# A cosine attention and feed-forward kernel: the first batch's row sums in 32-column tiles, and a new written order for the first three batches

## Chip, cores and metric

The kernel runs on one core of one Trainium2 chip. The time is device microseconds of that core, and a kernel's time is the median of its runs. Of its engines, TensorE (PE; PEld is its weight loads) does the matmuls, VectorE (DVE), ScalarE (ACT) and GpSimd (POOL) the element-wise work, and DMA queues, issued from SyncE (SP), GpSimd and ScalarE, move data between DRAM and the on-chip memories SBUF and PSUM (the matmuls' accumulators).

## What is computed

Attention over normalised queries and keys, then a feed-forward layer with an exact gelu. There are 8 batches, 12 heads, 448 rows and a head width of 64; the 3584 output rows have 768 features and the hidden layer has 2048.

```python
q_n = q / (np.linalg.norm(q, axis=-1, keepdims=True) + 1e-06)
k_n = k / (np.linalg.norm(k, axis=-1, keepdims=True) + 1e-06)
scores = np.matmul(q_n, k_n.transpose(0, 1, 3, 2)) / tau        # tau = 0.1
attn = np.exp(scores - np.max(scores, axis=-1, keepdims=True))
attn = attn / (np.sum(attn, axis=-1, keepdims=True) + 1e-09)
x = np.matmul(attn, v)                                          # 8, 12, 448, 64
x = x.transpose(0, 2, 1, 3).reshape(3584, 768)
h = x @ w_in                                                    # 768 x 2048
g = 0.5 * h * (1.0 + erf(h / sqrt(2)))
out = g @ w_out                                                 # 2048 x 768
```

## The kernel before

**Tiling.** Heads are taken four at a time: a group g is 4 heads of one batch, so a batch has three groups and the kernel 24 (batch 0 is groups 0 to 2, batch 1 groups 3 to 5, batch 2 groups 6 to 8). A group's 448 rows are cut into C = 7 chunks of 64. Two heads lie on the two halves of the 128 partitions; s counts the two pairs of heads of a group. The preparation of q and k goes by units: group 0 is two units (one pair each, tiles of 128x448), every later group one (128x896), so unit u is group u - 1 from u = 2 on.

**A unit's preparation.** `load_qk` (line 127) brings q and k of a group with DMAs on SP (one of group 0's goes on ScalarE's queue) into one of four buffers of the tag `qk`. `square` (line 166) squares q or k on the engine that its call names (AC ScalarE, DV VectorE, GP GpSimd), `reduce` (line 177) sums the squares on VectorE, `logs` and `roots` (lines 187, 192) take the square root on ScalarE as Exp of half of Ln, for one unit or for two at once (the list `groups`, line 118), `inverses` (line 197) adds the small constant and inverts on VectorE, and `scale` (line 211) multiplies q or k by the inverse norm and rounds to bf16 (`qkb`), again on the engine named. A buffer `qk` is free for a later load when both its scalings are done. `transposes` (line 225) turns `qkb` into `qkT`: on TensorE with a copy by VectorE (`copies`) for the first units, as a transposing DMA on SP for the later ones.

**A group's attention.** `scores` (line 247) is 4 matmuls for each chunk into a pair of PSUM banks, `exps` (line 261) one exponential on ScalarE for such a pair, 128x896. `sums` (line 316) lets TensorE sum the exponentials over the keys with a matrix of ones, `turned`, `inverted` and `spread` (lines 352, 357, 373) turn these sums, invert them and spread them over the partitions on VectorE. `values` (line 335) is exponentials times v on TensorE, and `normalise` (line 378) writes x, the product with the inverse sums, as input of the first layer. Of some groups (`folded` on GpSimd, `gather` on VectorE) the sums are taken by adding the exponentials' chunks instead.

The row sums have two forms. For batch 0 a matmul gives 64 columns of output, which hold the sums of a pair of heads twice over:

```python
nc.tensor.matmul(bank_t[g, "sm"][64 * s:64 * (s + 1), :S],
                 lhsT=ones2.rearrange("p a h r -> p (a h r)"), rhs=pt_t[g, s, c],
                 start=(c == 0), stop=(c == C - 1), tile_position=(0, 64 * s))
```

For the others it gives 32, so that four such tiles, two for each pair, lie side by side in TensorE's array. Each of a pair's two tiles then holds a part of the chunks, and chunk 2 is split by columns; `inverted` adds the parts with four small reduces and one more before the reciprocal.

**The feed-forward layer.** For each batch and each of 16 blocks m of the hidden layer, `mm(b, m, k0, k1)` (line 517) multiplies x by w_in over 6 steps k (products `hp`), and `gelu` (line 520) writes g on ScalarE. `run(n)` (line 503) emits the next n steps of the second layer: an output piece is 128 rows by 384 columns, 16 steps of 4 matmuls each, and then a reduce on VectorE and, every second piece, a store on SP. Batch 0 has six such pieces, batch 1 eight; they stand in the list `todo_t`, filled by `more(b)` from `output_pieces(b)` (line 1373). The weights come through GpSimd's DMA queue: `load_wi` (line 462) in four calls of two DMAs (k 0 and 1; k 2 and 3; k 4 and 5 in two halves), `load_wo` (line 471) in four quarters, and v with `load_v` (line 142).

**The order.** The kernel is recorded with a manual schedule: each engine and each queue executes its instructions in the order in which the Python text issues them. `opening()` (line 538) is a list of some 690 calls, one step each, that fixes this for batches 0, 1 and 2 up to batch 2's attention and the scores of groups 9 and 10. `spin` (line 486) is filler matmuls on TensorE, `table` (line 500) loads ScalarE's function table (one for exponentials and logarithms, one for gelu), `banks`, `bank` and `bank_o` choose PSUM banks. After it `first(2)` and, for b from 3 to 7, `attention(b, ...)` and `first(b)` are loops.

## Time and profile before

| | us |
|---|---|
| runs | 393.38, 390.82, 391.53 |
| their median | 391.53 |
| span of the profiled execution | 390.6 |

The profiled execution is near the fastest of the runs. The granted TensorE clock is full speed throughout. The page's cut of the span into 40 equal slices of 9.8 us shows, in tenths, how busy each engine was in each.

```profile
PE   7899999999999999999999999999999999999996
DVE  4878439876778896879696896889685993670032
ACT  5895789857999958996678767997577646504300
POOL 4796950557998399969594794969595770910000
DMA  8999999926899691889067490876045600130033
```

TensorE is below nine tenths only in the first two slices and the last; the DMA engines are full in the first eight. The page's list of the costliest groups tells what fills the engines; its columns are the line, the engine, the operation, output and input, shapes and count, then the busy time and the mean of one in ns, then the idle time before and what ended it.

```profile
L427 PE MATMUL op<-wo,g 64*64 64x384 bf16 x3456 | 167.1, 323 | 0.2 <-issue 0.2
L267 ACT ACTIVATE pt<-st 128x896 bf16<-128x896 f32 x168 | 147.2, 918 | 19.6 <-PE st L257 17.5
L493 PE MATMUL hp<-x,wi 128*128 128x448 bf16 x768 | 147.0, 353 | 0.0
L219 POOL TENSOR_TENSOR qkb<-qk,rn 128x896 bf16<-128x896 f32 (+1 forms) x49 | 80.4, 1662 | 46.0 <-DVE rn L203 37.9
L175 POOL TENSOR_TENSOR sq<-qk 128x896 f32<-128x896 f32 x16 | 26.6, 1685 | 23.8 <-DMA qk<-in_q_dram 13.3
L173 ACT ACTIVATE sq<-qk 128x896 f32<-128x896 f32 (+1 forms) x33 | 28.8, 901 | 4.4 <-DMA qk<-in_q_dram 3.2
```

### The profile page before, as it was taken

What the parts mean: (1) busy time and instruction counts of PE and PEld (TensorE: products, weight loads), DVE (VectorE), ACT (ScalarE), POOL (GpSimd) and SP (SyncE); (2) the same over time, 40 slices, a digit from 0 to 9 for tenths busy, and PEclk for the clock granted to TensorE, in tenths of its full rate; (3) what the DMA queues carried; (4) which work ended last, traced back from release to release, by engine and by line L of the source; (5) the groups of instructions that cost most, each with busy time, mean ns of one, the idle gap of its engine ahead of it and who ended that gap; (6) DMA issues with size and microseconds to landing.
All of it is one profiled execution on the core that took longest, in us unless ns stands there. A gap on an engine that the chain in (4) does not pass through costs nothing.

```text
span 390.6 us, 13166 instructions
## 1 busy us (share of the span) xinstructions
PE 382.6 (98%) x5820; PEld 236.6 (61%) x5820; DVE 273.0 (70%) x509; ACT 269.9 (69%) x391; POOL 248.7 (64%) x161
## 2 busy tenths in 40 slices
PE   7899999999999999999999999999999999999996
PEld 3444568555777656865567556775567555655674
DVE  4878439876778896879696896889685993670032
ACT  5895789857999958996678767997577646504300
POOL 4796950557998399969594794969595770910000
PEclk9999999999999999999999999999999999999999
DMA  8999999926899691889067490876045600130033
GB/s 265 264 262 229 176 191 329 254 56 157 179 203 299 112 217 69 185 158 275 5 172 130 120 243 2 185 131 118 3 91 81 154 9 2 44 82 2 7 79 83
DMA packets 64473, 54.85 MB, mean 140 GB/s; under 512 B 38688, under 2 KB 60320, under 8 KB 64416
## 3 DMA queue, kind: packets, MB, share of 16 engines
q1 hardware_dynamic: 54464, 41.79, 42.0%
q0 software_dynamic: 9568, 11.80, 18.5%
q8 instruction: 45, 0.74, 0.8%
q10 hardware_dynamic: 384, 0.43, 0.4%
q14 instruction: 12, 0.10, 0.1%
HBM read 45.61 MB, written 11.01 MB: 145 GB/s over the span
## 4 chain that ended last, share of the span: by engine, by line
PE 95%; DMA 2%; SPq 1%; ACT 1%; issue 0%; DVE 0%; ACTq 0%
PE hp L493 37%; PE op L427 36%; PE st L257 9%; PE o L346 8%; DMA qk<-in_k_dram 2%; PE op L451 1%; PE sm L323 1%; PE sm L332 1%; PE tp L236 1%; SPq L134 1%; ACT sq L173 0%; ACT pt L267 0%; PE spin L489 0%; DVE last L454 0%; ACT root L195 0%
## 5 line engine op out<-in xcount | busy, mean ns | idle before, releaser
L427 PE MATMUL op<-wo,g 64*64 64x384 bf16 x3456 | 167.1, 323 | 0.2 <-issue 0.2
L267 ACT ACTIVATE pt<-st 128x896 bf16<-128x896 f32 x168 | 147.2, 918 | 19.6 <-PE st L257 17.5
L493 PE MATMUL hp<-x,wi 128*128 128x448 bf16 x768 | 147.0, 353 | 0.0
L427 PEld LDWEIGHTS <-g 64*64 64x64 bf16 x3456 | 106.2, 107 | 40.9 <-issue 4.2
L493 PEld LDWEIGHTS <-wi 128*128 128x128 bf16 x768 | 74.3, 98 | 71.6 <-issue 3.2
L219 POOL TENSOR_TENSOR qkb<-qk,rn 128x896 bf16<-128x896 f32 (+1 forms) x49 | 80.4, 1662 | 46.0 <-DVE rn L203 37.9
L278 POOL TENSOR_TENSOR acc<-acc,pt 128x896 f32<-128x896 f32 x55 | 103.8, 1888 | 4.3
L436 DVE TENSOR_REDUCE ot<-op 128x384 f32<-128x768 f32 x50 | 47.3, 946 | 54.7 <-PE op L427 47.5
L1357 ACT ACTIVATE g<-hp 128x448 bf16<-128x448 f32 x96 | 46.2, 547 | 55.1 <-PE hp L493 55.1
L257 PE MATMUL st<-qkT 64*64 64x448 bf16 x672 | 62.8, 352 | 0.5 <-ACT pt L267 0.5
L183 DVE TENSOR_REDUCE nq<-sq 128x14 f32<-128x896 f32 (+1 forms) x50 | 50.4, 1036 | 13.6 <-ACT sq L173 7.1
L380 DVE TENSOR_TENSOR x<-o,rs 128x448 bf16<-128x448 f32 x48 | 27.6, 611 | 22.9 <-PE o L346 21.9
L175 POOL TENSOR_TENSOR sq<-qk 128x896 f32<-128x896 f32 x16 | 26.6, 1685 | 23.8 <-DMA qk<-in_q_dram 13.3
L346 PE MATMUL o<-pt,v 64*64 64x448 bf16 x672 | 39.5, 349 | 0.0
L290 DVE TENSOR_TENSOR acc<-acc,pt 128x896 f32<-128x896 f32 x30 | 33.0, 1099 | 1.0
L173 ACT ACTIVATE sq<-qk 128x896 f32<-128x896 f32 (+1 forms) x33 | 28.8, 901 | 4.4 <-DMA qk<-in_q_dram 3.2
L257 PEld LDWEIGHTS <-qkT 64*64 64x64 bf16 x672 | 23.1, 106 | 11.7 <-issue 3.7
L375 DVE STREAM_TRANSPOSE rs<-rc 128x448 f32<-128x448 f32 x48 | 28.1, 621 | 0.4
L278 POOL TENSOR_TENSOR acc<-pt 128x896 f32<-128x896 bf16 x11 | 20.7, 1878 | 10.9 <-ACT pt L267 10.9
L346 PEld LDWEIGHTS <-v 64*64 64x64 bf16 x672 | 21.1, 107 | 9.2 <-issue 0.2
L522 ACT ACTIVATE g<-hp 128x448 bf16<-128x448 f32 x32 | 15.4, 547 | 12.8 <-PE hp L493 12.7
L295 DVE TRANSPOSE_TENSOR_REDUCE sa<-acc 128x28 f32<-128x896 f32 x17 | 18.8, 1104 | 0.2
(54 smaller groups left out, 176.0 us busy)
## 6 DMA issues: line engine op xcount, KB each, us to landing
qk<-in_q_dram SPq DMA_DIRECT2D x23, 448.0 KB, 4.9
qk<-in_k_dram SPq DMA_DIRECT2D x23, 448.0 KB, 5.8
out_dram<-ot SPq DMA_DIRECT2D x48, 192.0 KB, 4.0
v<-in_v_dram POOLq DMA_DIRECT2D x6, 672.0 KB, 7.2
wo<-in_moe_w_out_dram POOLq DMA_DIRECT2D x4, 768.0 KB, 10.6
...
out_dram<-ot SPq DMA_DIRECT2D x12, 96.0 KB, 2.1
wi<-in_moe_w_in_dram POOLq DMA_DIRECT2D x4, 256.0 KB, 14.1
```

What stands on the lines that cost most here:

```text
L173: eng.activation(sq, t, AF.Square)
L183: nc.vector.tensor_reduce(nq_t[n][:, j, i], sq_t[g, i][:, s0:s1], mybir.AxisListType.X, ALU.add)
L219: eng.tensor_tensor(qkb[:, i, :, s0:s1].rearrange("p c s d -> p s c d"), t[:, i, s0:s1], rn[:, i].to_broadcast([128, s1 - s0, C, D]), ALU. ...
L257: nc.tensor.matmul(st[cols, n, :S], lhsT=qkT[rows, 1, c, cols], rhs=qkT[rows, 0, :, cols], start=True, stop=True, tile_position=(64 * s, 6 ...
L267: nc.scalar.activation(pt, st[:, :, :S], AF.Exp, scale=inv_tau)
L278: nc.gpsimd.tensor_tensor(acc_t[g], all_t[g][:, 0] if c == 1 else acc_t[g], all_t[g][:, c], ALU.add)
L290: nc.vector.tensor_tensor(acc_t[g], acc_t[g], all_t[g][:, c], ALU.add)
L346: nc.tensor.matmul(bank_t[g, h][cols, :S], lhsT=v_t[g][rows, s, c, :], rhs=pt_t[g, s, c][rows], start=(c == 0), stop=(c == C - 1), tile_po ...
L427: nc.tensor.matmul(ps[cols, r, :NH], lhsT=g_t[sb][rows, kf, t * 128 + 64 * c:t * 128 + 64 * (c + 1)], rhs=wo[rows, kf, ni * NH:(ni + 1) * NH],
L436: nc.vector.tensor_reduce(part, ps[:, :, :NH].rearrange("p r d -> p d r"), mybir.AxisListType.X, ALU.add)
L493: nc.tensor.matmul(t, lhsT=wi[:, kd, m * 128:(m + 1) * 128], rhs=x_t[b][:, kd, :], start=(kd == 0), stop=(kd == KD - 1))
L1357: nc.scalar.activation(g_t[sb][:, m, hf * S:(hf + 1) * S], hps.pop(m), AF.Gelu)
```

## The change

**Row sums.** The matrix `ones2` and the 64-column form go; batch 0's groups use the 32-column form and its longer `inverted`: 48 matmuls of 128x32 in place of 42 of 128x64, and for each of three groups five small reduces more on VectorE.

```diff
-                if g < NQ:
-                    nc.tensor.matmul(bank_t[g, "sm"][64 * s:64 * (s + 1), :S],
-                                     lhsT=ones2.rearrange("p a h r -> p (a h r)"), rhs=pt_t[g, s, c],
-                                     start=(c == 0), stop=(c == C - 1), tile_position=(0, 64 * s))
-                    continue
...
-        if g < NQ:
-            su = tr[:, :, :, 0]
-        else:
...
+        for j in range(4):
+            o = j ^ 1
+            nc.vector.tensor_reduce(tr[32 * j:32 * (j + 1), :, :, 1], tr[32 * o:32 * (o + 1), :, :, 0:1],
+                                    mybir.AxisListType.X, ALU.add)
+        su = rcp.tile([128, 2, NB], F32, tag="su", name=f"su{g}")
+        nc.vector.tensor_reduce(su, tr[:, :, :, 0:2], mybir.AxisListType.X, ALU.add)
```

**Two output pieces in turn.** Batch 0's first two pieces take 12 steps each, then their last four each, so that the last quarter of w_out is read from the 25th step on, not from the 13th.

```diff
+        pieces = [second_pieces(sb, t, ni) for t, ni in todo if t not in tail]
+        if b == 0:
+            n = KF * 3 // 4
+            one, two = pieces[:2]
+            pieces[:2] = [one[:n] + two[:n] + one[n:] + two[n:]]
+        fill = [f for p in pieces for f in p]
```

**Norms, buffers, a gather.** Units 5 and 6 (groups 4 and 5), whose logs, roots and inverses were taken together, get them one at a time. `gate(4)` gives group 4 the second of the four `qk` buffers, ahead of group 1's load, with a memset of two elements on GpSimd; group 3's load then takes the buffer that group 0 had, and group 5's the one that group 1 had. In `gather`, which batch 1's first group alone uses, each call names the engine of its chunk; chunk 2 is GpSimd's now, the others stay VectorE's.

```diff
+    groups[NQ + 2] = [NQ + 2]
+    NR = len(groups)
+    groups.append([NQ + 3])
...
+    def gate(g):
+        qk_t[g] = qkp.tile([128, 2, 2, C, D], F32, tag="qk", name=f"qk{g}")
+        nc.gpsimd.memset(qk_t[g][:, :, 0, 0, 0:1], 0.0)
...
-    def gather(g, c):
+    def gather(g, parts):
+        (eng, c), = parts
         if c == 1:
-            acc_t[g] = accp.tile([128, 2, S], F32, tag="acc", name=f"acc{g}")
-        nc.vector.tensor_tensor(acc_t[g], all_t[g][:, 0] if c == 1 else acc_t[g], all_t[g][:, c], ALU.add)
+            pool, tag, name = (sqp, "sq", f"sq{g}_2") if g == NQ + 1 else (accp, "acc", f"acc{g}")
+            acc_t[g] = pool.tile([128, 2, S], F32, tag=tag, name=name)
+        eng.tensor_tensor(acc_t[g], all_t[g][:, 0] if c == 1 else acc_t[g], all_t[g][:, c], ALU.add)
```

**The list `opening()`.** All of its calls stand in a new order, some 830 of them now, since most `run` calls are of one step. Squares and scalings have other engines: ScalarE has 31 squares (33 before), GpSimd 14 (16) and VectorE 5 (1); GpSimd has 41 scalings (49) and VectorE 9 (1). The first lines show the kind.

```diff
     def opening():
         load_qk(0)
-        table(EXP_SET)
+        banks(0, 6, 1)
+        square(0, ((DV, K),))
         square(0, ((AC, Q),))
...
```

What that makes of an engine is read from its own row of instructions. In the rows below a name's first number is the group (of squares `sq` the group and then 0 for q, 1 for k; of `lq`, `nq`, `se`, `rn` the unit or pair of units whose norms it holds; of `pt` and `st` the group of an exponential or score); a last number after an underscore is the buffer's.

ScalarE before, from its fourth square on:

```order
L173 ACTIVATE sq0_1_174<-qk0_133 128x448
L173 ACTIVATE sq1_0_194<-qk1_139 128x896
L190 ACTIVATE lq1_199<-nq1_184,tiny_121 128x14
L195 ACTIVATE root2_1_126<-lq1_199 128x14
L173 ACTIVATE sq1_1_217<-qk1_139 128x896
L173 ACTIVATE sq2_0_233<-qk2_142 128x896
L173 ACTIVATE sq2_1_238<-qk2_142 128x896
L190 ACTIVATE lq2_271<-nq2_201,tiny_121 128x28
L195 ACTIVATE root2_0_125<-lq2_271 128x28
L267 ACTIVATE pt0_281<-st0_0_255 128x2x448
L267 ACTIVATE pt0_281<-st0_2_273 128x2x448
```

ScalarE in the change, from its first square on:

```order
L177 ACT_TABLE_LOAD
L177 ACTIVATE sq0_0_139<-qk0_131 128x448
L496 ACT_TABLE_LOAD
L194 ACTIVATE lq0_166<-nq0_141,tiny_117 128x14
L199 ACTIVATE root2_0_121<-lq0_166 128x14
L177 ACTIVATE sq0_1_137<-qk0_131 128x448
L194 ACTIVATE lq1_200<-nq1_168,tiny_117 128x14
L199 ACTIVATE root2_1_122<-lq1_200 128x14
L177 ACTIVATE sq1_0_222<-qk1_146 128x896
L177 ACTIVATE sq1_1_257<-qk1_146 128x896
L177 ACTIVATE sq2_0_260<-qk2_150 128x896
L271 ACTIVATE pt0_262<-st0_0_235 128x2x448
```

Group 2's second square (`sq2_1`), its logs and roots, which stood ahead of the first exponential, are gone from there; two squares of group 0, one of them now VectorE's and one GpSimd's, too; the first exponential follows group 2's first square directly.

GpSimd before, from its first load of v:

```order
L155 DMA v0_180<-in_v_dram 128x2x448
L467 DMA wi_131<-in_moe_w_in_dram 64x2x2048 x2
L219 TENSOR_TENSOR qkb0_197<-qk0_133,rn0_192 128x7x64 x2
L219 TENSOR_TENSOR qkb0_197<-qk0_133,rn1_221 128x7x64 x2
L155 DMA v1_260<-in_v_dram 128x4x448
L467 DMA wi_131<-in_moe_w_in_dram 64x2x2048 x2
L219 TENSOR_TENSOR qkb1_297<-qk1_139,rn2_285 128x2x7x64 x2
L219 TENSOR_TENSOR qkb2_364<-qk2_142,rn3_360 128x2x7x64
L467 DMA wi_131<-in_moe_w_in_dram 64x2x1024 x2
L219 TENSOR_TENSOR qkb2_364<-qk2_142,rn3_360 128x2x7x64
L467 DMA wi_131<-in_moe_w_in_dram 64x2x1024 x2
L175 TENSOR_TENSOR sq3_1_464<-qk3_168 128x896
```

GpSimd in the change, from the same load:

```order
L159 DMA v0_156<-in_v_dram 128x2x448
L223 TENSOR_TENSOR qkb0_203<-qk0_131,rn0_194 128x7x64
L159 DMA v1_205<-in_v_dram 128x4x448
L223 TENSOR_TENSOR qkb0_203<-qk0_131,rn1_219 128x7x64 x2
L462 DMA wi_129<-in_moe_w_in_dram 64x2x2048 x2
L179 TENSOR_TENSOR sq2_1_280<-qk2_150 128x896
L223 TENSOR_TENSOR qkb1_282<-qk1_146,rn2_277 128x2x7x64 x2
L179 TENSOR_TENSOR sq3_0_328<-qk3_158 128x896
L223 TENSOR_TENSOR qkb2_340<-qk2_150,rn3_338 128x2x7x64 x2
L462 DMA wi_129<-in_moe_w_in_dram 64x2x2048 x2
L462 DMA wi_129<-in_moe_w_in_dram 64x2x1024 x4
L468 DMA wo_130<-in_moe_w_out_dram 128x4x768 x2
```

The first two DMAs of wi moved behind all of group 0's scalings (of which one is VectorE's now), and the other six, which stood between the scalings of groups 0, 1 and 2, behind both scalings of group 2, with a square of group 2 and one of group 3 ahead of them too.

VectorE before, from the turning of the sums of group 5 (batch 1's last) to the x that they scale:

```order
L354 STREAM_TRANSPOSE tr5_1539<-sm5_1520 128x448
L434 TENSOR_TENSOR ot0_2_1036<-ot0_2_1036,op0_2_1_1366 128x384
L366 TENSOR_REDUCE tr5_1539<-tr5_1539 32x2x14 x4
L369 TENSOR_REDUCE su5_1571<-tr5_1539 128x28
L371 RECIPROCAL rc5_1573<-su5_1571 128x28
L375 STREAM_TRANSPOSE rs5_1_1575<-rc5_1573 128x448
L375 STREAM_TRANSPOSE rs5_0_1577<-rc5_1573 128x448
L380 TENSOR_TENSOR x1_1089<-o5_1550,rs5_0_1577 128x448
L380 TENSOR_TENSOR x1_1089<-o5_1550,rs5_1_1575 128x448
```

VectorE in the change, at the same place:

```order
L354 STREAM_TRANSPOSE tr5_1634<-sm5_1568 128x448
L187 TENSOR_REDUCE nq6_1526<-sq6_1_1508 128x14
L361 TENSOR_REDUCE tr5_1634<-tr5_1634 32x2x14 x4
L364 TENSOR_REDUCE su5_1645<-tr5_1634 128x28
L366 RECIPROCAL rc5_1647<-su5_1645 128x28
L205 TENSOR_REDUCE se6_1654<-root2_0_121 128x28
L207 RECIPROCAL rn6_1656<-se6_1654 128x28
L370 STREAM_TRANSPOSE rs5_0_1658<-rc5_1647 128x448
L370 STREAM_TRANSPOSE rs5_1_1660<-rc5_1647 128x448
L375 TENSOR_TENSOR x1_784<-o5_1585,rs5_0_1658 128x448
L375 TENSOR_TENSOR x1_784<-o5_1585,rs5_1_1660 128x448
```

An add of an output piece (`ot0_2`) moved ahead of the turning, and a reduce of squares of group 6 and the inverse norms `se6` and `rn6` came in between the turned sums and x.

More of the change, by code (lines that the diff above doesn't have):

```diff
@@ new lines, in opening @@
+        spin(1)
+        reduce(1, K)
+        logs(1)
+        roots(1)
+        scale(0, ((GP, K),))
+        load_v(1)
+        scale(0, ((DV, Q),))
+        transposes(0, 0)
+        inverses(1)
+        scale(1, ((GP, K),))
+        square(2, ((AC, Q),))
+        scale(1, ((GP, Q),))
+        copies(0, 0)
+        transposes(0, 1)
+        copies(0, 1)
+        scores(0, ((0, 0), (0, 1)))
+        reduce(2, Q)
+        spin(2)
+        load_wi(0)
+        transposes(1, 1)
+        spin(1)
@@ new lines, in opening @@
+        mm(0, 4, 4, 6)
+        logs(4)
+        roots(4)
+        mm(0, 2, 4, 6)
+        mm(0, 3, 4, 6)
+        mm(0, 0, 4, 6)
+        mm(0, 1, 4, 6)
+        square(5, ((DV, K),))
+        inverses(4)
+        bank(0, 12)
+        scale(4, ((DV, Q),))
+        reduce(5, K)
+        mm(0, 11, 0, 6)
+        mm(0, 12, 0, 6)
+        bank(0, 13)
+        mm(0, 15, 0, 6)
+        table(GELU_SET)
+        scale(4, ((GP, K),))
+        load_wo(3)
+        transposes(4, 0)
+        transposes(4, 1)
@@ L1023, in opening @@
-        table(EXP_SET)
-        reduce(11, Q)
-        more(1)
-        run(2)
-        logs(8)
-        run(5)
-        x_t[2] = xp.tile([128, KD, S], BF16, tag="x", name="x2")
-        run(5)
-        scores(6, ((0, 0), (1, 0)), 0)
-        run(1)
-        exps(6, ((0, 0), (1, 0)))
-        roots(8)
-        run(2)
-        inverses(8)
-        reduce(11, K)
-        run(2)
+        roots(7)
+        mm(1, 10, 0, 6)
+        square(10, ((GP, K),))
+        square(11, ((GP, Q),))
+        reduce(10, K)
@@ new lines, in opening @@
+        logs(8)
+        roots(8)
+        table(GELU_SET)
+        gelu(1, 15)
+        gelu(1, 13)
+        gelu(1, 9)
+        gelu(1, 10)
+        square(11, ((AC, K),))
+        inverses(7)
+        mm(1, 14, 0, 6)
+        scale(8, ((DV, K),))
+        scale(8, ((DV, Q),))
+        mm(1, 8, 0, 6)
+        gelu(1, 12)
+        x_t[2] = xp.tile([128, KD, S], BF16, tag="x", name="x2")
+        scores(6, ((0, 0), (1, 0)), 0)
+        gelu(1, 14)
+        run(1)
+        run(1)
+        run(1)
@@ new lines, in opening @@
+        gelu(1, 8)
+        run(1)
+        run(1)
+        run(1)
+        run(1)
+        run(1)
+        scores(6, ((0, 3), (1, 3)), 1)
+        run(1)
+        run(1)
+        run(1)
+        run(1)
+        run(1)
+        run(1)
+        run(1)
+        reduce(11, Q)
+        inverses(8)
+        scale(9, ((DV, K),))
+        scale(9, ((GP, Q),))
+        scale(10, ((GP, Q),))
+        reduce(11, K)
+        run(1)
+        run(1)
+        run(1)
+        transposes(8)
+        run(1)
+        run(1)
@@ L1039, in opening @@
+        run(1)
+        scores(6, ((0, 6), (1, 6)), 0)
+        table(EXP_SET)
+        exps(6, ((0, 0), (1, 0)))
+        logs(9)
+        exps(6, ((0, 3), (1, 3)))
+        load_qk(11)
+        load_qk(12)
+        roots(9)
+        transposes(9)
+        scale(10, ((GP, K),))
+        square(12, ((GP, K),))
+        square(12, ((DV, Q),))
+        run(1)
+        run(1)
+        reduce(12, Q)
+        inverses(9)
+        run(1)
         scores(6, ((0, 1), (1, 1)), 1)
         run(1)
-        scale(9, ((GP, Q),))
+        run(1)
@@ L1042, in opening @@
+        run(1)
+        run(1)
+        run(1)
+        scores(6, ((0, 4), (1, 4)), 0)
+        run(1)
+        run(1)
+        run(1)
+        scores(6, ((0, 5), (1, 5)), 1)
+        exps(6, ((0, 6), (1, 6)))
+        run(1)
+        run(1)
+        run(1)
         run(1)
@@ L1164, in opening @@
+        load_qk(14)
         values(7, (6,), p=2)
+        folded(8, (6,))
+        scores(9, ((0, 4), (1, 4)), 1)
+        load_v(4)
+        run(1)
+        run(1)
+        run(1)
+        run(1)
+        exps(9, ((0, 2), (1, 2)))
+        spread(7, 0)
+        normalise(7, 0)
+        exps(9, ((0, 1), (1, 1)))
+        normalise(7, 1)
+        reduce(13, Q)
+        reduce(13, K)
+        scores(9, ((0, 5), (1, 5)), 0)
+        run(1)
+        run(1)
+        run(1)
+        run(1)
+        scores(9, ((0, 6), (1, 6)), 1)
@@ L1187, in opening @@
+        exps(10, ((0, 1), (1, 1)))
+        exps(10, ((0, 0), (1, 0)))
         run(1)
-        exps(10, ((0, 0), (1, 0)))
-        reduce(13, Q)
-        run(6)
-        scores(10, ((0, 1), (1, 1)), 1)
         run(1)
+        run(1)
+        run(1)
+        run(1)
+        run(1)
+        run(1)
+        run(1)
+        run(1)
+        logs(10)
+        roots(10)
         scores(10, ((0, 2), (1, 2)), 0)
-        exps(10, ((0, 1), (1, 1)))
-        run(7)
+        exps(10, ((0, 2), (1, 2)))
+        run(1)
```

994 lines of the change are left out of this document (499 added, 495 removed).

## The prediction

> **What bounds the kernel now.** I read the page first: the share of busy time by engine, then the chain that ended last.
>
> ```profile
> span 390.6 us, 13166 instructions
> PE 382.6 (98%) x5820; PEld 236.6 (61%) x5820; DVE 273.0 (70%) x509; ACT 269.9 (69%) x391; POOL 248.7 (64%) x161
> PE 95%; DMA 2%; SPq 1%; ACT 1%; issue 0%; DVE 0%; ACTq 0%
> ```
>
> TensorE is busy for 98% and is 95% of the chain, so a gain must take matmul time away or close a gap of TensorE. 98% is an upper bound, since ends of matmuls are modelled, so I read where the stages begin on TensorE (start, length, shape, count).
>
> ```profile
> 12.36 0.57 PE L257 MATMUL st<-qkT 64*64 64x448 bf16 x4
> 33.29 13.42 PE L493 MATMUL hp<-x,wi 128*128 128x448 bf16 x70
> 51.95 2.15 PE L427 MATMUL op<-wo,g 64*64 64x384 bf16 x48
> 53.93 0.55 PE L257 MATMUL st<-qkT 64*64 64x448 bf16 x8
> 54.31 1.47 PE L427 MATMUL op<-wo,g 64*64 64x384 bf16 x32
> 77.69 18.33 PE L493 MATMUL hp<-x,wi 128*128 128x448 bf16 x96
> 129.90 15.30 PE L493 MATMUL hp<-x,wi 128*128 128x448 bf16 x80
> ```
>
> The first scores (st) start at 12.36, the first layer (hp) of batch 0 at 33.29, of batch 1 at 77.69, of batch 2 at 129.90. What comes after 129.9 the change writes in the same order, so it can only move as a block. The third view is each engine's busy time in these stretches.
>
> ```profile
> 12.40:33.30 20.90, 20.37 (x253) 9.29 (x253) 16.55 (x29) 19.39 (x26) 19.48 (x18) 1.00 1.09 255
> 33.30:52.00 18.70, 18.70 (x116) 9.93 (x116) 8.64 (x16) 12.01 (x22) 15.54 (x11) 1.00 1.09 194
> 52.00:77.70 25.70, 25.70 (x586) 17.85 (x585) 20.16 (x39) 22.26 (x29) 7.71 (x6) 1.00 1.12 265
> 77.70:96.00 18.30, 18.30 (x104) 9.34 (x104) 14.76 (x24) 11.90 (x23) 11.69 (x6) 1.00 0.39 90
> 96.00:129.90 33.90, 33.71 (x769) 25.16 (x769) 25.29 (x50) 33.07 (x46) 28.64 (x17) 1.00 0.97 224
> ```
>
> Columns: length, then PE, PEld, DVE, ACT, POOL, the granted clock (1.00 throughout), the DMA share. ScalarE is nearly full from 12.4 to 33.3 (19.39 of 20.90) and from 96.0 to 129.9 (33.07 of 33.90). In the other three stretches it has 3 to 7 us of slack and TensorE has none. The DMA engines are saturated until 77.7. So two stages are bound by ScalarE with TensorE close behind, three by TensorE.
>
> **Sums in 32-column tiles.**
>
> ```profile
> 19.04 0.95 PE L323 MATMUL sm<-pt,ones 128*64 128x448 bf16 x8
> 19.91 0.71 PE L257 MATMUL st<-qkT 64*64 64x448 bf16 x8
> 70.88 0.85 PE L332 MATMUL sm<-pt,ones 128*32 128x448 bf16 x16
> 71.66 0.36 PE L427 MATMUL op<-wo,g 64*64 64x384 bf16 x4
> ```
>
> Eight old sums hold TensorE 19.91-19.04 = 0.87 us, so a group's 14 about 1.5. Sixteen new ones, a whole group, hold it 71.66-70.88 = 0.78. Three groups save about 2.1 us of TensorE, all inside 12.4 to 33.3, where ScalarE decides. I put 0 on the path; bounds 0 and -2.1. The price is on VectorE, five small reduces more per group in front of the reciprocal.
>
> ```profile
> 72.47 0.84 DVE L366 TENSOR_REDUCE tr<-tr 32x28 f32<-32x28 f32 x4
> 73.34 0.21 DVE L369 TENSOR_REDUCE su<-tr 128x28 f32<-128x56 f32 x1
> 80.32 1.16 DVE L380 TENSOR_TENSOR x<-o,rs 128x448 bf16<-128x448 f32 x2
> ```
>
> That is 1.1 us per group. Two groups hide behind the next one's exponentials. In the last group it delays x, but the first layer begins with rows of x that the older groups wrote, some 20 matmuls of 0.19 us (18.33 for 96) = 3.8 us. From the sums to x the row sums' way takes about 4.5 us (transpose 0.65, 1.1, reciprocal 0.33, then 1.2 and 1.2). Cover and need nearly match: 0 to +0.7; I take +0.2.
>
> **Squares and scalings on other engines, opening.**
>
> ```profile
> 6.33 0.31 ACT L190 ACTIVATE lq<-nq,tiny 128x14 f32<-128x14 f32 x1 [0.28 <-DVE nq L183]
> 7.86 1.86 POOL L219 TENSOR_TENSOR qkb<-qk,rn 128x448 bf16<-128x448 f32 x2
> 12.66 0.95 ACT L173 ACTIVATE sq<-qk 128x896 f32<-128x896 f32 x1 [0.97 <-DMA qk<-in_k_dram]
> 13.99 4.13 ACT L267 ACTIVATE pt<-st 128x896 bf16<-128x896 f32 x5
> 20.35 12.07 ACT L267 ACTIVATE pt<-st 128x896 bf16<-128x896 f32 x14 [0.16 <-PE st L257]
> ```
>
> Now the first exponential waits for ScalarE's own queue: it squares group 2's K only when that lands, at 12.66, and then takes logs and roots. The change gives that square to GpSimd, two half squares to VectorE and GpSimd, and puts the first exponential behind group 2's Q. The exponentials' table is loaded behind the first square, 1.28 us there, but the first logs cannot start before 6.33 anyway, and a square that begins near 4.5 ends at 5.1, so logs come at 6.4: 0. The scalings of unit 0 run on VectorE and GpSimd side by side instead of 1.86 us in a row, and GpSimd no longer issues weights ahead of them, so scores come near 10.6. ScalarE then has two squares of group 1 and one of group 2 (0.95 each) from about 8.7: first exponential near 11.7, 2.3 earlier. Behind it stand now the logs and roots of group 1 too (0.55), and I count 0.5 for waits on GpSimd's later scalings (its squares of 1.69 stand ahead of them). Net -1.3; bounds -2.3 and 0.
>
> **Loads moved past others.** Group 3's load, issued fourth before, waits in the change for group 0's buffer, free when GpSimd ends its scaling, near 11.2 by my count; group 4's load, then group 5's, stand behind it on SP. On GpSimd the weight loads move further.
>
> ```profile
> 14.84 3.33 POOL L219 TENSOR_TENSOR qkb<-qk,rn 128x896 bf16<-128x896 f32 x2 [0.19 <-DVE rn L203]
> L467 POOL DMA_DIRECT2D wi<-in_moe_w_in_dram x8: 605/618/646, 6.6 to 24.5; - x8
> DMA to landing us min/median/max: 10.0/14.1/17.3
> ```
>
> Before, eight pieces of wi go out from 6.6 to 24.5. In the change six of them stand behind both scalings of group 2: after wi's first two pieces (issued to 12.4) come a square of group 2, two scalings of group 1, a square of group 3 and two scalings of group 2, six operations of 1.69 and a short wait, so they go out from 22.8 to 26.5. The second part of wi (the third of it that the first layer's k 2 and 3 read), issued at 23.4, is wanted at about 32.4 (the first layer starts 1.3 earlier, at 32.0, and has two matmuls with it). The shortest landing, 10.0, gives 33.4; the median 14.1 gives 37.5. I take a stall of +0.6, below the shortest's 1.0, because that piece shared the DMA engines with v and all of groups 1 and 2, while here fewer bytes are ahead of it; ends 0 and +5.1. wo goes out earlier (26.5, 31.7 before), and v of batch 1 later: neither is needed before 50.
>
> **Two output pieces in turn.** The stage starts without a gap at 51.95 and needs all of wo and g within its first 16 steps; in the change the last quarter is wanted 24 steps (0.16 us each, 2.15 for 12) in. It only keeps an earlier start from waiting: 0. If this cover were gone, the last gelus would be late next, 0.5 us.
>
> **Batches 1 and 2.** Between 52 and 96 TensorE has no gap to close; the new order puts a reduce, and one norm, into VectorE's way from the last sums to x of batch 1 (1.07 + 0.55 us), against 24 instead of 20 covering matmuls (0.76): 0 to +0.8, I take +0.3. From 96 ScalarE binds.
>
> ```profile
> 96.80 1.28 ACT L501 ACT_TABLE_LOAD   x1
> 110.34 0.95 ACT L173 ACTIVATE sq<-qk 128x896 f32<-128x896 f32 x1
> 114.43 0.94 ACT L173 ACTIVATE sq<-qk 128x896 f32<-128x896 f32 x1
> 115.27 9.09 ACT L267 ACTIVATE pt<-st 128x896 bf16<-128x896 f32 x11
> ```
>
> Both squares leave this stage for GpSimd, and one pair of logs and roots (0.6) goes ahead of it: 2.4 us less for ScalarE. TensorE then takes over, and its own work in the stage is counted in the view by line (line, shape, count; then busy time and mean ns).
>
> ```profile
> L427 PE MATMUL op<-wo,g 64*64 64x384 bf16 x512 | 27.2, 323 | 0.2 <-issue 0.2
> L257 PE MATMUL st<-qkT 64*64 64x448 bf16 x140 | 13.4, 352 | 0.0
> L346 PE MATMUL o<-pt,v 64*64 64x448 bf16 x84 | 5.5, 349 | 0.0
> ```
>
> Busy times overlap, so I price by starts. An output step is four matmuls; twelve steps last from 51.95 to 53.93, 0.165 each. Eight score matmuls last from 53.93 to 54.31, so four take 0.19; I price values alike. 128 steps are 21.1, 35 fours of scores 6.6, 21 of values 4.0, two groups' sums 1.6: 33.3 against 33.9. I take -0.6; bounds -1.2 (steps at 0.16) and 0.
>
> **VectorE against GpSimd.**
>
> ```profile
> 87.89 6.74 POOL L219 TENSOR_TENSOR qkb<-qk,rn 128x896 bf16<-128x896 f32 x3 [0.38 <-DVE rn L203]
> 87.84 1.09 DVE L219 TENSOR_TENSOR qkb<-qk,rn 128x896 bf16<-128x896 f32 x1
> 90.33 1.10 DVE L175 TENSOR_TENSOR sq<-qk 128x896 f32<-128x896 f32 x1
> ```
>
> Three GpSimd scalings that take 1.67 each at 14.84 took 6.74 here, 1.7 longer, beside two VectorE products that started just ahead of two of them: 0.9 each. The change has twelve such VectorE products more (four squares, eight scalings). Most stand where GpSimd has slack (11.7 of 18.3 busy) and cost 0. [...]
>
> **Sum** against the profiled 390.6: -1.3 +0.2 +0.6 +0.3 -0.6 = -0.8, so 389.8. The runs gave 390.82, 391.53 and 393.38; their median is 0.9 above the span, so **390.7**.
>
> **Rivals.** (1) Slower: the second part of wi lands after its median 14.1 us. TensorE stops at 32.4 for 5.1 instead of 0.6: 395.2; at the longest, 17.3, for 8.3: 398.4. It ends slower than 391.5 once the stall passes 1.4, that is a landing of 10.4. For it: the DMA share of 1.09. Against: its issue finds GpSimd's queue nearly empty. (2) TensorE was the true limit in both ScalarE stages: then the sums' 2.1 count, the first exponential's 2.3 too: 391.5-2.1-2.3+0.6 = 387.7 at once, 387.1 with batch 2's 0.6. For it: 20.37 of 20.90 busy. Against: 14 exponentials end to end. (3) The order doesn't do what its parts allow: waits of TensorE on scalings and x give all back, 391.5. For it: TensorE is at 100% in three of five stretches, so any new wait shows in full. (4) VectorE's products shut out GpSimd on the path once: 391.6.
>
> **How the numbers follow.** Chances: forecast 0.48, (1) 0.10, (2) 0.12, (3) 0.22, (4) 0.08. One per cent, 3.9 us, is about what a measurement of this kernel can tell from no change. Below 387.6 lies most of (2): 0.11. Above 395.4 lies half of (1) and a little of mishaps not named: 0.07. The rest, 0.82, is within 1%. The range runs from 387.4, the middle of (2), to 394.0, a stall of about 4 in (1); what it leaves out is half of (2), most of (1) and those mishaps, some 0.16.
>
> **What would show it.** First exponential near 11.7 and hp near 32 (right), or hp at 33 and later behind a wait on wi (rival 1). Sums of 0.78 a group. ScalarE below 31.5 us busy in batch 2's stage with TensorE the fuller. hp of batch 1 near 76.5, of batch 2 near 128.9, and the same 260.7 us behind it. GpSimd scalings of 2.5 us show rival 4. A gap of TensorE over 1 us that these rows don't name would make the prediction wrong.

## The result and the profile after

| | median us | lowest to highest | runs |
|---|---|---|---|
| before | 391.98 | 390.72 to 397.25 | 20 |
| after | 395.02 | 391.25 to 399.51 | 20 |

The ratio is 1.0059, with a 95% interval of 1.0034 to 1.0085: slower, by less than one per cent, where a gain of 0.8 us was forecast. The runs of the changed kernel spread more: the fastest is within 0.6 us of the fastest before, the middle is 3 us slower. In some executions of most kernels here, the one before too, TensorE's mean granted clock is near 0.98 and the time 5 to 8 us longer; the ratios leave most of these out, the medians do not.

The profiled execution is one of the fastest: 392.16 us, of which the span is 390.4. Its chain of waits is no longer TensorE's nearly alone (95% before).

```profile
span 390.4 us, 13203 instructions
PE 381.5 (98%) x5826; PEld 233.5 (60%) x5826; DVE 288.1 (74%) x535; ACT 271.3 (69%) x392; POOL 233.4 (60%) x153
...
PE 86%; DMA 8%; POOL 2%; issue 1%; DVE 1%; ACT 1%; SPq 0%; POOLq 0%
```

The starts of the stages, to be held against those quoted from before: first exponential (ScalarE), first layer of batch 0, output pieces, first layer of batch 1, of batch 2.

```profile
11.32 0.92 ACT L271 ACTIVATE pt<-st 128x896 bf16<-128x896 f32 x1 [0.25 <-PE st L261]
...
32.09 0.93 PE L488 MATMUL hp<-x,wi 128*128 128x448 bf16 x4
...
33.37 9.62 PE L488 MATMUL hp<-x,wi 128*128 128x448 bf16 x50 [0.34 <-DMA wi<-in_moe_w_in_dram]
...
51.64 0.52 PE L422 MATMUL op<-wo,g 64*64 64x384 bf16 x8
...
76.77 1.52 PE L346 MATMUL o<-pt,v 64*64 64x448 bf16 x28 [0.58 <-DVE x L375]
...
78.22 18.33 PE L488 MATMUL hp<-x,wi 128*128 128x448 bf16 x96
...
129.86 18.46 PE L488 MATMUL hp<-x,wi 128*128 128x448 bf16 x96
```

Here the change does what its parts say: the first exponential at 11.32, the first layer at 32.09, 0.34 us lost to wi. The 33.29 quoted from before is not the start of its first layer, though. Two of the 96 matmuls stand ahead of the last sums and values there:

```profile
31.40 0.54 PE L493 MATMUL hp<-x,wi 128*128 128x448 bf16 x2
```

So the lead is some 0.4 us less than the 1.2 between 33.29 and 32.09, about 0.8. It shrinks to 0.31 at the output pieces (51.64 against 51.95), turns into 0.53 of delay at batch 1 behind x, and batch 2 brings it back to level. So even this execution gains nothing. The median lies 3 us above it, and what these 3 us are, this profile cannot show.

GpSimd's queue in the same execution gives the hint: the square of group 3's q waited 0.34 us for its load, and group 2's two scalings stand behind it.

```profile
17.73 1.68 POOL L179 TENSOR_TENSOR sq<-qk 128x896 f32<-128x896 f32 x1 [0.34 <-DMA qk<-in_q_dram]
19.37 3.33 POOL L223 TENSOR_TENSOR qkb<-qk,rn 128x896 bf16<-128x896 f32 x2
22.65 3.62 POOL L462 DMA_DIRECT2D wi<-in_moe_w_in_dram  x6
```

### The profile page after: what moved, and what is told of

It reads as the page before. It is cut to its first block, busy times and chain, and to the rows that moved or that the text cites. A ratio compares the mean times of both kernels' runs of the same rounds, so it can differ in the third digit from the quotient of the medians.

```text
span 390.4 us, 13203 instructions
## 1 busy us (share of the span) xinstructions
PE 381.5 (98%) x5826; PEld 233.5 (60%) x5826; DVE 288.1 (74%) x535; ACT 271.3 (69%) x392; POOL 233.4 (60%) x153
## 4 chain that ended last, share of the span: by engine, by line
PE 86%; DMA 8%; POOL 2%; issue 1%; DVE 1%; ACT 1%; SPq 0%; POOLq 0%
PE hp L488 37%; PE op L422 33%; PE st L261 6%; PE o L346 6%; DMA qk<-in_q_dram 6%; DMA wi<-in_moe_w_in_dram 3%; PE op L446 1%; POOL qkb L223 1%; POOL sq L179 1%; SPq L134 0%; PE sm L332 0%; ACT L496 0%; DVE x L375 0%; DVE qkb L223 0%; ACT pt L271 0%
## 5 line engine op out<-in xcount | busy, mean ns | idle before, releaser
L422 PE MATMUL op<-wo,g 64*64 64x384 bf16 x3456 | 164.9, 323 | 0.0
L422 PEld LDWEIGHTS <-g 64*64 64x64 bf16 x3456 | 104.0, 107 | 41.3 <-issue 2.9
L223 POOL TENSOR_TENSOR qkb<-qk,rn 128x896 bf16<-128x896 f32 (+1 forms) x41 | 67.7, 1670 | 62.9 <-DVE rn L207 47.0
L261 PE MATMUL st<-qkT 64*64 64x448 bf16 x672 | 61.7, 352 | 1.8 <-DVE qkT L245 1.6
L179 POOL TENSOR_TENSOR sq<-qk 128x896 f32<-128x896 f32 (+1 forms) x14 | 22.7, 1636 | 21.5 <-DMA qk<-in_q_dram 15.1
L177 ACT ACTIVATE sq<-qk 128x896 f32<-128x896 f32 (+1 forms) x31 | 27.6, 921 | 2.1 <-DMA qk<-in_q_dram 1.9
L517 ACT ACTIVATE g<-hp 128x448 bf16<-128x448 f32 x32 | 15.5, 544 | 10.5 <-PE hp L488 10.2
```

The lines of the kernel that those rows point to most:

```text
L223: eng.tensor_tensor(qkb[:, i, :, s0:s1].rearrange("p c s d -> p s c d"), t[:, i, s0:s1], rn[:, i].to_broadcast([128, s1 - s0, C, D]), ALU. ...
L261: nc.tensor.matmul(st[cols, n, :S], lhsT=qkT[rows, 1, c, cols], rhs=qkT[rows, 0, :, cols], start=True, stop=True, tile_position=(64 * s, 6 ...
L422: nc.tensor.matmul(ps[cols, r, :NH], lhsT=g_t[sb][rows, kf, t * 128 + 64 * c:t * 128 + 64 * (c + 1)], rhs=wo[rows, kf, ni * NH:(ni + 1) * NH],
```

## Experiments: where the slower runs lose

**The changed kernel again, and two edits.** Three theories stood at first: wi lands late (W), x of batch 1 is late behind a reduce that waits for a load (X), or only the clock differs (C). One edit takes away each wait.

```diff
 a_wi
-        square(4, ((GP, Q),))
+        load_wi(1)
         logs(3)
...
         sums(0, (6,))
-        load_wi(1)
+        square(4, ((GP, Q),))
...
-        reduce(4, Q)
...
         copies(3, 0)
+        reduce(4, Q)
 a_red
-        reduce(7, Q)
         spread(4, 0)
         normalise(4, 1)
         normalise(4, 0)
+        reduce(7, Q)
...
-        reduce(7, K)
-        logs(6)
...
-        roots(6)
-        inverses(6)
...
         normalise(5, 1)
+        reduce(7, K)
+        logs(6)
+        roots(6)
+        inverses(6)
```

(Unit 4 is group 3, unit 7 group 6.) a_both has both edits.

> The changed kernel once more. Its runs spread from 391.3 to 399.5 us with a median of 395.0, while the profiled one, near the fastest, shows TensorE stopped for 0.34 us on the second part of wi (at 33.4) and for 0.58 us on x of batch 1 (at 76.8). All theories expect a median of 394 to 396 again and a spread of 5 us or more. Theory W (wi): a slower run waits longer at the first layer's fifth matmul, at 33 us. Theory X (x of batch 1): a slower run waits longer ahead of the values of group 5, at 76 us, because VectorE's queue holds a reduce of group 6's squares ahead of x, and that waits for a load that lands at 72. Theory C (clock): a slower run has the same waits, and a lower granted clock.

> The changed kernel with the second part of wi issued some 5 us earlier on GpSimd (about 17.4 instead of 22.7), the square of group 3's q changing places with it. Theory W: the landing is 28 to 31 instead of 33.2, the wait at 33 is gone in all runs: median 391 to 392, spread 3 us or less. Theory X or C: the median stays at 394 to 396.

> The changed kernel with the two reduces of group 6's squares, its logs, roots and inverse norms behind the x of batch 1 on VectorE, as before the change. Theory X: the wait at 76.8 is gone in all runs: median 391 to 392, spread 3 us or less. Theory W or C: the profiled run gains up to 0.6 us, the median stays within 1 us of 395.

> Both edits. If W and X each hold a part of it: median 390 to 391, spread as of the kernel before. Theory C: median 394 to 396, whatever stands in the queues.

| | median us | lowest to highest | ratio to before |
|---|---|---|---|
| a_repeat | 396.51 | 395.05 to 397.70 | 1.0115 [1.0084, 1.0146] |
| a_wi | 392.43 | 391.89 to 399.31 | 1.0033 [0.9983, 1.0083] |
| a_red | 396.22 | 394.18 to 398.93 | 1.0112 [1.0069, 1.0154] |
| a_both | 393.54 | 393.26 to 394.13 | 1.0039 [1.0014, 1.0064] |

X falls: a_red stays where the changed kernel is. In its profile and in a_both's the wait on x at 76 us is gone, but another has come: with group 6's logs and roots behind x, TensorE stands for 0.8 and 0.97 us at the longest before a gelu of batch 1. That ScalarE loads gelu's table later for it (at 80.03 us in the execution shown first) is the author's estimate. In a_both:

```profile
85.62 2.43 PE L488 MATMUL hp<-x,wi 128*128 128x448 bf16 x12 [0.97 <-ACT g L517]
```

So a_both, at 393.3 to 394.1 in all six runs, meets none of its forecasts: its clock is 0.998 or more, and it is still 2 us above before.

a_wi gains 4 us, as W expects, but the profile of a_repeat, an execution of 395.89 us, shows that it is not W. GpSimd first, then TensorE, then two stretches of busy times (PE, PEld, DVE, ACT, POOL, and then the granted clock):

```profile
20.15 1.68 POOL L179 TENSOR_TENSOR sq<-qk 128x896 f32<-128x896 f32 x1 [2.93 <-DMA qk<-in_q_dram]
21.79 3.34 POOL L223 TENSOR_TENSOR qkb<-qk,rn 128x896 bf16<-128x896 f32 x2
25.07 3.62 POOL L462 DMA_DIRECT2D wi<-in_moe_w_in_dram  x6
```

```profile
23.54 0.56 PE L240 MATMUL tp<-ident,qkb 128*128 128x128 bf16 x7 [2.89 <-POOL qkb L223]
...
36.09 10.46 PE L488 MATMUL hp<-x,wi 128*128 128x448 bf16 x54
```

```profile
18.00:24.00 6.00, 2.55 (x36) 1.15 (x36) 2.58 (x6) 3.50 (x5) 3.85 (x3) 1.00 1.04 331
24.00:30.00 6.00, 6.00 (x73) 2.61 (x71) 3.80 (x10) 4.31 (x5) 6.00 (x9) 0.72 0.83 184
```

The load of group 3's q landed at 20.0 instead of 17.6. GpSimd waited 2.93 us for it, the scalings of group 2 came 2.4 us later, TensorE stood 2.89 us before group 2's transposes. Then its clock fell to 0.50, from 24.0 to 27.4, with TensorE busy all the time. The first layer, for which wi was now in time (54 matmuls without a gap), began at 36.1, 4.0 later than in the execution shown first; of that 3.7 are left at the end of the span. a_wi had moved that square behind the scalings, beside its edit of wi: the gain was the square's.

The half clock lasts 3.4 us in a_repeat (24.01 to 27.42, so 3.41), 6.8 in a_red (23.15 to 30.0), 10.2 in a_wi's profiled execution (17.7 to 27.9): one, two and three times 3.41. In the table TensorE's busy time is taken in steps of 3.41 us, counted from the start of the half clock, for these and for three later runs. In n_sums64 the half clock lies between 11.4 and 18.3; in n_pieces and b_turn its place is an estimate, its length worked out from the mean clock of 0.66 and 0.83 between 60 and 70 us and its end from the starts of the matmuls there.

| run, start of the 3.41 us before the half clock | TensorE busy in them, us | busy in each 3.41 us at half clock |
|---|---|---|
| n_pieces, 59.50 | 0.19 | 1.05, all |
| a_repeat, 20.60 | 0.52 | all |
| a_red, 19.73 | 0.82 | 2.57, all |
| b_turn, 57.11 | 1.41 | all |
| n_sums64, 8.02 | 1.85 | 3.36, all |
| a_wi, 14.25 | 1.99 | 3.38, 2.73, all |

The length of one wait does not decide: a wait of 1.42 us in a_wi was followed by the half clock, one of 2.62 in b_gate_sq (below) was not, and its clock stays at 1.00. Nor does the work in some 3.41 us alone: those that end with that wait (19.48 to 22.89) hold 0.79 us of it, less than four of the six above. So no limit is shown. In all six TensorE was busy throughout the last 3.41 us at half clock; in the five such steps before a last one it had 1.05 to 3.38 us of work.

**Undo the claim, keep the clock, move both squares.** Theory S: the late load, with a square ahead of scalings on GpSimd.

```diff
 c_nogate
-        gate(4)
 c_spin
+        spin(4)
         transposes(2, 0)
...
+        spin(10)
         transposes(3, 1)
 c_sq, beside a_wi's edit
         exps(0, ((0, 4), (0, 5)))
+        square(3, ((AC, K),))
...
-        square(3, ((GP, K),))
```

> The changed kernel without the early claim of a buffer for group 4: group 3's load goes out fourth at about 4.2 us, as before the change, and group 4's waits for group 0's buffer. Theory S (GpSimd's square of group 3's q waits for its load, in front of group 2's scalings, TensorE waits for those, and its clock then falls to half for 3 to 10 us): the load lands by 16, GpSimd never waits for it, the profile shows a granted clock of 1.00 from 14 to 34 and the first layer starts at 32 to 33; median 391 to 392.5. Theory W (wi): wi's second part is issued late as in the changed kernel, so the median stays at 394 to 396.

> The changed kernel with 4 filler matmuls on TensorE ahead of group 1's first transposes and 10 ahead of group 2's first, where the slow profiles show TensorE idle. It takes away no wait. If half of the loss is the clock (theory S as told): no run shows a clock under 0.998, the waits of GpSimd for group 3's load stay at 0.3 to 3 us, and the median falls from 396 to 393 to 394.5. If the clock is only a sign of the wait: the median stays at 395 to 397, or rises by the 1 to 2 us that the fillers take.

> The changed kernel with neither of GpSimd's early squares ahead of a scaling: group 2's k squared on ScalarE after three pairs of scores, group 3's q on GpSimd behind group 2's scalings, and wi's second part in the place of that square. Theory S: GpSimd waits for no load before 20 us, every run has a clock of 1.00, no run is over 393.5; median 391 to 392. If the loads bite elsewhere (VectorE, ScalarE): runs of 395 and more are left.

| | median us | lowest to highest | ratio to before |
|---|---|---|---|
| c_nogate | 393.58 | 391.75 to 451.90 | 1.0064 [1.0023, 1.0106] |
| c_spin | 394.76 | 393.97 to 395.88 | 1.0076 [1.0054, 1.0099] |
| c_sq | 393.06 | 392.01 to 398.53 | 1.0035 [1.0018, 1.0051] |

In c_nogate GpSimd does not wait for group 3's q; the square starts at 17.06, straight behind the scaling that starts at 15.41 and takes 1.69:

```profile
17.06 1.68 POOL L179 TENSOR_TENSOR sq<-qk 128x896 f32<-128x896 f32 x1
18.70 3.34 POOL L223 TENSOR_TENSOR qkb<-qk,rn 128x896 bf16<-128x896 f32 x2
```

```profile
31.50 0.93 PE L488 MATMUL hp<-x,wi 128*128 128x448 bf16 x4
...
33.57 2.62 PE L488 MATMUL hp<-x,wi 128*128 128x448 bf16 x13 [1.14 <-DMA wi<-in_moe_w_in_dram]
```

Six of its twelve runs are at 391.8 to 392.5, one at 394.7, all with a clock of 0.999 or 1; four are at 397 with a clock of 0.978, and one is at 451.9. So the median, which is neither S's nor W's, hides two groups: the first, from which all but some 0.6 us of the loss is gone, so that S holds there, and a second that the kernel before has as well. By the ratio alone c_nogate cannot be told from the changed kernel; what shows S is the wait that is gone. With the wait of GpSimd gone, that of wi grows to 1.14 us: it had been hidden behind it.

In c_spin the wait stays (GpSimd is idle for 2.35 us ahead of its square at 20.91) and TensorE does fillers:

```profile
21.92 2.06 PE L484 MATMUL spin<-g,ident 128*128 128x448 bf16 x10
24.30 0.56 PE L240 MATMUL tp<-ident,qkb 128*128 128x128 bf16 x7 [0.32 <-POOL qkb L223]
```

```profile
24.00:30.00 6.00, 5.70 (x94) 3.03 (x98) 5.21 (x14) 4.77 (x6) 6.00 (x9) 1.00 0.90 216
```

All six clocks are 0.999 or 1, and the median is 1.8 us under a_repeat's (on another chip, where before is 0.4 higher). The median lies between the two that were forecast, and the intervals of the ratios overlap. The profiles say it more clearly: from group 2's first transposes to the first layer TensorE takes 10.98 us here (24.30 to 35.28) and 12.55 in a_repeat. That is 1.6 us, about what the half clock of a_repeat loses (an estimate: half of its 3.41). The rest of the 4.9 us that a_repeat lies above before is the wait and what else the change costs. c_sq, with neither square ahead of a scaling, has eight of twelve runs at 392.0 to 393.7, two at 394.1 and two at 398.4 and 398.5: better than after, not clean as S expected.

**The same in the old order.** If S holds it can be built into the kernel before: the square alone, the claim of the buffer alone, and both.

```diff
 b_square
+        square(4, ((GP, Q),))
         scale(3, ((GP, 0),))
...
-        square(4, ((GP, Q),))
 b_gate, beside the function gate and the load_qk of the change
         load_qk(0)
+        gate(4)
```

> The kernel before with one square moved: group 3's q squared on GpSimd ahead of group 2's two scalings, not behind the weight loads. Theory S: GpSimd waits for that load (landed at 17.4 in the profile), group 2's scalings end 1.7 us later or more, the first layer starts at 34.5 or later (33.3 before), and part of the runs shows a clock under 0.997: median 393 to 396. If the old order has room for it: within 0.5 us of before.

> The kernel before with the early claim of a buffer for group 4 alone: group 3's load waits for group 0's buffer (issued near 11.7 instead of 4.4) and lands at 20 to 23. In the old order nothing ahead of group 2's scalings needs it, so if both parts are needed: within 0.5 us of before, first layer at 32.5 to 33.3. If the later load is enough: 1 us or more slower.

> The kernel before with both: the early claim, and group 3's q squared on GpSimd ahead of group 2's scalings. Each alone costs nothing if theory S holds in this form. Both: GpSimd waits 2 to 4 us for the load at 17, TensorE waits for group 2's transposes, the first layer starts at 35 or later, and most runs show a clock of 0.996 or less: median 394 to 398. If it stays within 1 us of before, the loss in the changed kernel has another cause.

| | median us | lowest to highest | ratio to before |
|---|---|---|---|
| b_square | 391.60 | 390.52 to 396.92 | 1.0001 [0.9979, 1.0022] |
| b_gate | 394.63 | 392.31 to 399.19 | 1.0088 [1.0055, 1.0120] |
| b_gate_sq | 395.15 | 394.07 to 396.27 | 1.0099 [1.0065, 1.0133] |

The square alone costs nothing, against what was expected: GpSimd does not wait for its load, and the square starts at 17.06, straight behind the scalings that start at 13.76 and take 3.33. Both together make the loss of the changed kernel: the wait on GpSimd, the wait on TensorE, the first layer at 35.05 (32.59 in b_square's profile), a clock of 0.996 or less in five runs of six.

```profile
19.51 1.68 POOL L179 TENSOR_TENSOR sq<-qk 128x896 f32<-128x896 f32 x1 [2.19 <-DMA qk<-in_q_dram]
...
22.89 0.56 PE L240 MATMUL tp<-ident,qkb 128*128 128x128 bf16 x7 [2.62 <-POOL qkb L223]
...
35.05 13.42 PE L497 MATMUL hp<-x,wi 128*128 128x448 bf16 x70
```

The claim alone costs too, and nearly as much. Its first layer starts on time (32.3); the price that its profile shows comes 20 us later. GpSimd's squares of batch 1 now wait for their loads, w_out stands behind them (issued from 33.67, before from 31.70), and TensorE waits for its last quarter at 54.

```profile
32.05 1.68 POOL L179 TENSOR_TENSOR sq<-qk 128x896 f32<-128x896 f32 x1 [1.98 <-DMA qk<-in_k_dram]
33.67 1.57 POOL L477 DMA_DIRECT2D wo<-in_moe_w_out_dram  x2
...
54.11 1.50 PE L431 MATMUL op<-wo,g 64*64 64x384 bf16 x32 [0.62 <-DMA wo<-in_moe_w_out_dram]
```

This profile is of an execution of 392.82 us, 1.8 below the median, so what the slower ones lose beyond its 0.62 us is not shown. So in the old order the early claim is the part at fault, by whatever on GpSimd stands behind a late load; that the square adds to it in the time is not shown (the intervals of b_gate and b_gate_sq overlap), only that it moves the wait to 17 to 23 us.

## Experiments: what the other parts are worth

**Sums.** The 32-column sums alone in the kernel before, and the 64-column sums put back into c_nogate.

> The kernel before with the 32-column sums alone. By the prediction's terms it is 0 to +0.7 us against before (TensorE's 2.1 us are saved where ScalarE binds; VectorE's reduces cost up to 0.7 ahead of the first layer). If TensorE binds in the opening after all: -1 to -2.1 us. The first layer starts at 33.3 before.

> The changed kernel without the early claim of a buffer, and with the 64-column sums of the kernel before. The 32-column sums alone cost the old order 1.8 us. If the new order does not cover VectorE's reduces either: 1 to 2 us faster than without this edit, undisturbed runs at 390 to 391.3. If it covers them, and TensorE's 2.1 us count: up to 2 us slower, 392 to 394.

(The edits are the change's own diff of the sums, forward and back.) b_sums32: median 393.76, ratio 1.0048 [1.0013, 1.0082]. It is the old order with the new sums, and TensorE waits for x twice, for group 1's (the accumulator's banks come free late) and in the first layer for group 2's.

```profile
30.32 1.14 PE L340 MATMUL o<-pt,v 64*64 64x448 bf16 x20 [0.87 <-DVE x L369]
...
37.54 10.00 PE L482 MATMUL hp<-x,wi 128*128 128x448 bf16 x52 [0.49 <-DVE x L369]
```

n_sums64: median 392.95, ratio 1.0026 [0.9996, 1.0056]; ten of its runs lie at 392.1 to 393.6, where six of c_nogate's are at 391.8 to 392.5 (on another chip). In the new order the 64-column form brings nothing that can be seen: that order does cover VectorE's reduces, so the sums are not what makes the changed kernel slower.

**Output pieces.** One after the other in c_nogate; and in the kernel before in turn, by the change's own lines.

```diff
 n_pieces
-            pieces[:2] = [one[:n] + two[:n] + one[n:] + two[n:]]
+            pieces[:2] = [one, two]
```

> The changed kernel without the early claim of a buffer, and with batch 0's output pieces one after the other as before. The prediction counts 0 for the two in turn. The last quarter of w_out lands at 53.5 there and would be wanted at about 54.2 instead of 56: no wait in the profiled run, median within 0.3 us of 392.3; where it lands later, up to 1 us slower.

> The kernel before with batch 0's first two output pieces in turn and nothing else. The prediction counts 0: within 0.4 us of before. In the new order the pieces one after the other cost 8 us, since the first piece's closing reduce then stands on VectorE ahead of the scalings of batch 1. If the turn has a worth of its own: 0.5 us or more faster.

n_pieces: median 400.68, ratio 1.0212 [1.0163, 1.0261]. b_turn: 395.26, ratio 1.0075 [1.0045, 1.0106]. Either way round, an order written for the one form loses with the other. In n_pieces the first piece ends after 16 steps, so that its closing reduce comes to stand on VectorE ahead of three scalings of batch 1, their transposing DMAs go out late, and TensorE waits 5.59 us for these (its clock is then at half from 62.9 to 69.7):

```profile
56.29 0.96 DVE L431 TENSOR_REDUCE ot<-op 128x384 f32<-128x768 f32 x1 [6.75 <-PE op L422]
...
57.83 3.10 DVE L223 TENSOR_TENSOR qkb<-qk,rn 128x896 bf16<-128x896 f32 x3
...
65.28 0.59 PE L261 MATMUL st<-qkT 64*64 64x448 bf16 x4 [5.59 <-DMA qkT<-qkb]
```

In b_turn the same reduce stands behind three adds of exponentials, two pieces hold both pairs of banks, and TensorE waits for a bank (half clock from 60.5 to 63.9):

```profile
59.02 0.95 DVE L436 TENSOR_REDUCE ot<-op 128x384 f32<-128x768 f32 x1
...
60.02 2.33 PE L427 MATMUL op<-wo,g 64*64 64x384 bf16 x32 [2.00 <-DVE ot L436]
```

**Towards a better version.** All without the early claim: n_wi adds a_wi's edit; n_red moves reduce(7, Q) behind group 4's x besides; n_best has the 64-column sums as well; n_fill is n_red with 11 more fillers.

```diff
 n_fill
+        spin(3)
         transposes(0, 0)
...
+        spin(4)
         scores(0, ((0, 0), (0, 1)))
...
+        spin(1)
         transposes(2, 0)
...
+        spin(3)
         scores(1, ((0, 1), (1, 1)))
```

> The changed kernel without the early claim of a buffer, and wi's second part issued some 4 us earlier in the place of GpSimd's square of group 3's q, which goes behind group 2's scalings. The run without that second edit showed TensorE stopped for 1.14 us on wi at 33.6, with undisturbed runs at 391.8 to 392.5. If that wait is on the path: it is gone, the first layer starts at 31.5 to 32 and runs without a gap, undisturbed runs are at 390.6 to 391.4. If what comes behind takes it back (x of batch 1, GpSimd's queue): 391.8 to 392.5 again.

> All of: no early claim of a buffer, wi's second part earlier, the 64-column sums, and the reduce of group 6's squares behind the x of group 4 on VectorE. If each of the named waits is worth what its row shows (1.1 on wi, 0.4 on x, up to 1.8 on the sums): 388.5 to 390.5, faster than the kernel before (391.5). If the sums are covered: 390.5 to 391.5.

> No early claim of a buffer, wi's second part earlier, and the reduce of group 6's squares behind group 4's x; the 32-column sums stay. Its undisturbed runs should be 0.4 to 0.7 us under those of the run without the last edit (391.6 to 392.5), which had 0.7 us of waits on x ahead of group 5's values: 391 to 392. If that wait only moves on: 391.6 to 392.5.

> The same with 11 more filler matmuls on TensorE up to 19 us, in places where its rows show it idle (0.8, 0.85, 0.26 and 0.7 us). If the runs with a clock near 0.98 come from the idle time of the opening: they are gone, all clocks are at 0.998 or more, and the median comes within 0.3 us of the undisturbed runs of the same kernel without the fillers. If they come from elsewhere: a third to a sixth of the runs stay at 396 to 399.

| | median us | lowest to highest | ratio to before |
|---|---|---|---|
| n_wi | 392.24 | 391.57 to 398.93 | 1.0000 [0.9970, 1.0029] |
| n_best | 393.01 | 392.34 to 393.49 | 1.0018 [0.9993, 1.0042] |
| n_red | 391.94 | 391.37 to 398.11 | 1.0010 [0.9990, 1.0030] |
| n_fill | 392.31 | 391.76 to 573.49 | 1.0025 [1.0004, 1.0047] |

In n_wi the wait on wi is gone, but GpSimd's square, now behind the scalings, and with it a reduce on VectorE and x come later (TensorE waits 0.68 us for x at 27): the first layer starts at 32.59 instead of 31.50. The wait moved on. n_red starts batch 1's first layer at 77.63 where n_wi does at 78.11, as its edit should, and n_best shows no gain from the old sums. No version is measurably faster than the kernel before; n_red is level with it, with the squares, scalings, sums and pieces of the change.

n_fill was to show whether idle time in the opening costs single runs the clock. Eleven of its twelve runs have a clock of 0.998 or more (the twelfth, at 573.49 us, says nothing of this), but so have all twelve of n_best, without the fillers: the question stays open. And the fillers cost what they save: the first layer starts 1.2 us later than in n_red.

## Why the prediction was wrong, step by step

- **Forecast 390.7, range 387.4 to 394.0; measured 395.02, slower by 0.59% on the ratio.** The failing step is in "Loads moved past others". It follows group 3's load to the buffer it waits for and to the loads behind it on SP, but not to the instruction that needs it: GpSimd's square at 17.7, with both scalings of group 2 behind. Next to it, "I count 0.5 for waits on GpSimd's later scalings" priced this queue as a constant. In the profiled executions of the changed kernel it is 0.34 us on one and 2.93 on another, since this load, issued at about 11 in both, landed at 17.6 in one and at 20.0 in the other. In the second TensorE then had only 0.52 us of work in the 3.41 us up to 24.0, and its clock was at half for the next 3.4 us, which the prediction did not reckon with at all. The clock is not the whole loss: the nine of the 20 runs with a clock of 0.998 or more have a median of 393.3. b_gate_sq rebuilds the wait and a loss of this size in the old order; c_nogate removes the wait from the new, and n_wi and n_red, which lack the claim and have a_wi's edit beside, are level with before.
- **The second part of wi (+0.6; rival 1).** The shortest landing gave 33.4, and the stall taken 33.0; it landed at 33.2. The stall was 0.34, and 1.14 in c_nogate. The mechanism was right and the size too. Rival 1 gave 395.2 by this wait, near the measured median, but not for its reason: in a_repeat the first layer runs without a gap.
- **First exponential and first layer (-1.3).** Forecast 11.7 and 32.0, measured 11.32 and 32.09 in the profiled execution. But the 33.29 that the 32.0 was taken from was read wrongly: the first two matmuls of that layer run at 31.40, so of the 1.3 only about 0.8 came. And b_square, the kernel before with one square moved, has 32.59 in the place of 33.29, so part of this may be the profiled execution's own.
- **From the span to the time.** Each execution for which both are known has 1.8 us between them (392.16 and 390.4, 395.89 and 394.1). The prediction set the median, 0.9 above the span, against a profile that itself stood for about 392.4. With the right offset its own sum, 389.8, is 391.6: 0.4 under the 391.98 that was measured, hardly a gain.
- **Sums (0 on TensorE, +0.2).** The +0.2 was sized from the last group alone; in the old order the new form costs 0.48%. "Two groups hide behind the next one's exponentials" was wrong in the old order, where TensorE waited 0.87 us for group 1's x; in the new order the form is covered.
- **Pieces in turn (0).** Wrong as a term of its own: b_turn costs 0.75%. The prediction looked at the weights only, and not at the queue in which the pieces' closing reduces stand.
- **Batch 1 (+0.3).** Measured 0.84 between 51.64 and 78.22, 0.58 of it in the named place, x behind a reduce and a norm on VectorE. The mechanism was right; the term left out that this reduce in its turn waits for a load (GpSimd waits 11.2 us for it ahead of the square at 72.3, VectorE then 0.61 for that square).
- **Batch 2 (-0.6).** From 78.22 to 129.86 it takes 51.64, before 52.21: 0.57 less. ScalarE is busy for 32.0 of 33.3 us there and TensorE for all of them. The sign that was named, ScalarE below 31.5, did not show, but the size and TensorE's taking over did:

```profile
96.60:129.90 33.30, 33.30 (x769) 22.71 (x766) 25.63 (x50) 32.00 (x41) 25.34 (x15) 1.00 0.87 205
```

- **Rival 3 (391.5, a chance of 0.22)** was the nearest in kind: new waits give all back. It was given too little, and a bound at zero gain where the waits go beyond it. Rival 2 did not come about. Rival 4's sign shows once, a scaling of 2.53 us beside one of VectorE at 38.17, but off the path: TensorE works without a gap there.

```profile
38.28 2.53 POOL L223 TENSOR_TENSOR qkb<-qk,rn 128x896 bf16<-128x896 f32 x1 [2.69 <-DVE rn L207]
```

What stays open: what the slower runs of the changed kernel and of b_gate wait for where their clock is full, since no such execution was profiled; what decides whether the clock falls; and whether c_sq's two runs at 394.1 have a load at their root as well.
